# Attention, a Fourier mix and an MLP on one core: a second place for batch 0's scores, earlier transposes, another order of loads and weight sums

## The chip, the cores and the metric

The kernel runs on one core of one Trainium2 chip. The metric is the device time of one execution in microseconds (us), given as the median of several executions. A profile is taken of one execution; its times are counted from the start of that execution's span. The engines are PE (TensorE matmul, with PEld for its weight loads), DVE (VectorE), ACT (ScalarE), POOL (GpSimd) and SP (SyncE, which here issues DMAs only).

## The reference

The inputs are q, k and v of 4 batches, 8 heads, 768 positions and 64 channels, 8 memory keys and values for each head, and the two weights of an MLP. First comes attention in chunks, then a mix over positions and channels by Fourier transforms, then a normalised MLP:

```python
for c in range(768 // 32):                       # chunks of 32 queries
    k_ctx = k[:, :, max(0, 32*c - 16):min(768, 32*c + 40)]
    k_full = concat([mem_k, k_ctx]); v_full = concat([mem_v, v_ctx])
    a = softmax(q_c @ k_full.T / 8)
    out[:, :, chunk c] = a @ v_full
x = out as (4, 768, 512)
u = x + real(fft(fft(x, axis=1), axis=2))
un = (u - mean(u)) / sqrt(var(u) + 1e-6)
return u + relu(un @ w_ch1) @ w_ch2              # 512 -> 2048 -> 512
```

## The kernel before

**Work and tiles.** The heads are taken in pairs, n = 0 to 15, four pairs to a batch (`seq`, L250). One pair goes through these steps in `attention(n)` (L941):

- `e_load_qk` (L340) loads q and k from POOL's DMA queue and casts them to bf16, into one of three stage tiles `qs`, `ks` (L236, chosen by n modulo 3). `e_load_v` (L352) loads v from SP's queue into one of four tiles `va`, with a group of DMAs for each head: L362 for both heads' first keys, L358 for the others, L367 for the memory values. The tiles `va` have an edge set to zero and ones (`e_edges`, `e_edge_ones`) and low rows set to zero (`e_low_rows`, L329, an ACT copy).
- For batches 0 to 2, PE transposes q (`e_turn_q`, 16 matmuls of line L377 into the PSUM tile `trq`) and k (`e_turn_k`, into `trk`). `e_qT` (L393, ACT) copies the first to SBUF and `e_kT` (L412, line L420: DVE for pairs 0 to 3, ACT for 4 to 11) the second into `kTb`; `e_mkT` (L408) puts the memory keys there. For batch 3 DMA transposes do this.
- Each pair has two halves g. `e_scores` (L426, 12 matmuls of L433) writes the PSUM tile `sc`, of which there is one, two banks large. `e_exp` (L437, two ACT instructions of L441) reads it. `e_values` (L445, 24 matmuls of L457) multiplies with v into `xa` (g = 0) or a bank `xo` (g = 1). `e_norm` (L461, two DVE instructions, L467 and L468) divides and writes the batch's tile `xsb`.

After batch 0's pairs, `first_fourier` (L1071) makes folded sums on DVE (`g_zy` L599, `g_ff` L610 and others), splits them into high and low parts (L651 on ACT, L655 on DVE) and multiplies them with cosine and sine tables (L675, L688). `columns_of` (L1171) transforms the columns (L699), adds them to the batch's tile (`e_sum`, L705), takes mean and variance (L713, L714) and normalises (`e_un`). The MLP follows in tiles of 256 rows: first layer L775 with `e_relu` (L784), second layer L793, or for batches 2 and 3 a form with seven products of quarters instead of eight (L842) that needs sums of W2's quarters (`e_w2t`, L809 to L817, DVE).

**Order of the work.** All instructions are made as tasks of a planner (`Plan`, L37) and written out in the order that it finds. A task has an engine, an assumed cost, tasks that it comes after, PSUM banks or buffers that it takes and gives back, and a rank. At each planned moment each engine takes the ready task of lowest rank; without a rank of its own a task has its number, so batch 0's attention and its Fourier work come ahead of later pairs. `behind` holds a task until another has been placed. PE's costs are doubled before the planned time `WARM` (L44). The order is then fixed: on the chip each engine runs its list in order and waits where the data isn't there.

While PE has nothing ready, from the first scores up to the first low part of the Fourier work (L1120), the planner puts in products of zeros (`e_fill`, L899, matmul L902). They write a PSUM bank of their own, one of the two `mlp` banks. The PSUM banks in all: `tr` (1), `xa` (1), `sc` (2), `acc` (2), `mlp` (2).

**POOL's queue.** In order of rank: loads of pairs 0 to 2, memsets of the last rows of `ks` 1 and 2 (L885), masks, edges and ones of `va` 2 and 3, memsets of `kU` (L939), q and k of pair 3, and then a gate, a copy of one element of pair 3's v of head 1 (`e_gate`, L956), behind which the loads of pair 4 stand. The loads of W1 (L1062) come after pair 5's, those of W2 (L1067) after pair 6's.

Of the kernel before, what the change touches and what calls it, by code (L numbers as in the profile page):

```python
# [10 lines left out]
FP32 = mybir.dt.float32  # L11
# [25 lines left out]
class Plan:  # L37
# [6 lines left out]
    WARM = 18.0  # L44
# [47 lines left out]
    def order(self):  # L92
# [9 lines left out]
        while any(waiting.values()):  # L102
# [5 lines left out]
            for e, ts_ in waiting.items():  # L108
# [49 lines left out]
                else:  # L158
                    if e == "PE" and self.filling and self.filling[0]["at"] is not None \
                            and self.filling[1]["at"] is None:  # L160
                        cost = self.FILL * (2.0 if now < self.WARM else 1.0)
                        idle[e] = now + cost
                        placed.append(dict(engine="PE", cost=cost, emit=self.fill, at=now,
                                           done=now + cost))
                        moved = True
# [12 lines left out]
def kernel(  # L178
# [38 lines left out]

    bank_of, bank_free = {}, {"acc": [0, 1], "mlp": [0, 1]}

    def bank(tag, shape, dtype, name):  # L220
        i = bank_free[tag].pop(0)
        t = fps.tile(shape, dtype, tag=f"{tag}{i}", bufs=1, name=name)
        bank_of[name].append((t, tag, i)) if name in bank_of else bank_of.update({name: [(t, tag, i)]})
        return t
# [12 lines left out]
    ks = [spool.tile([P, 2, RB * D], BF16, name=f"ks{i}") for i in range(NS)]  # L237
    NV = 4
# [90 lines left out]
    def e_low_rows(i):  # L329
        low = va[i][0:MEM0].rearrange("p h t c -> p (h t c)")  # L330
        nc.scalar.copy(low, zero[0:MEM0].to_broadcast([MEM0, 2 * NT * 66]))
# [8 lines left out]
    def e_load_qk(n, i):  # L340
        b, pr = seq[n]
        src, dst = ((q, qs), (k, ks))[i]
        if b >= TURNED:
            for hh in range(2):
                nc.gpsimd.dma_start(
                    strided(dst[n % NS], hh * D, [[2 * D, NST], [1, D]]),
                    src[b, 2 * pr + hh].rearrange("(a p) d -> p a d", p=P))
            return
        nc.gpsimd.dma_start(dst[n % NS][0:QP],
# [30 lines left out]
    def e_flip_q(n):  # L380
        qT_of[n] = qT = apool.tile([P, S], BF16, tag="qT", bufs=2, name="qT")
        nc.sync.dma_start_transpose(qT.rearrange("p (a s) -> p a s", s=P),
                                    qs[n % NS].rearrange("p h c -> p (h c)")[:, 0:S])

    def e_flip_k(n):
        nc.sync.dma_start_transpose(kU[n % NKU][:, KR:KR + S].rearrange("p (a s) -> p a s", s=P),
                                    ks[n % NS].rearrange("p h c -> p (h c)")[:, 0:S])

    def e_turn_q(n):
        tr_of[n] = trq = aps.tile([P, S], BF16, tag="tr", bufs=1, name="trq")  # L390
        turn(trq, qs[n % NS][0:QP], ident_b[0:QP, 0:QP])

    def e_qT(n):  # L393
        qT_of[n] = qT = apool.tile([P, S], BF16, tag="qT", bufs=2, name="qT")
        nc.scalar.copy(qT.rearrange("p (a j) -> p a j", j=RB),  # L395
                       tr_of.pop(n).rearrange("p (j a) -> p a j", j=RB))

    def e_turn_k(n):
        if n < HP:
            trk = bank("acc", [P, RB * KP], BF16, "trk")  # L400
        else:
            trk = aps.tile([P, RB * KP], BF16, tag="tr", bufs=1, name="trk")
        tr_of[n, 1] = trk
        turn(trk, ks[n % NS][0:KP], turn_b)
# [21 lines left out]
    def e_scores(n, g):  # L426
        qT, kT = qT_of[n], kTb[n % NKT]
        sc_of[n, g] = sc = aps.tile([P, 2, 8, 64], FP32, tag="sc", bufs=1, name="sc")
# [448 lines left out]
    def e_idb():  # L877
# [7 lines left out]
    t_kzs = add("POOL", 1.0, lambda: [nc.gpsimd.memset(ks[i][QP:KP], 0.0) for i in range(1, NS)],  # L885
                rank=14)
    t_low, LOW = {}, 110
    for i in range(NV):
# [3 lines left out]
        t_low[i] = add("ACT", 1.45, lambda i=i: e_low_rows(i), [t_zero, e_],  # L892
                       rank=(0, 1, 2, 3)[i])
    t_masks = add("POOL", 0.6, e_masks, rank=16)
    dz = cpool.tile([P, P], BF16)
    fill_of = []
    t_dz = add("DVE", 0.15, lambda: nc.vector.memset(dz, 0.0), rank=-30)

    def e_fill():  # L899
        if not fill_of:  # L900
            fill_of.append(bank("mlp", [P, 512], FP32, "idle"))
        nc.tensor.matmul(fill_of[0][:, 0:384], dz, strided(dz, 0, [[0, 3], [1, P]]),  # L902
                         start=True, stop=True)

    t_fill = add("PE", 0.33, e_fill, [t_dz], take=("mlp",), rank=-1)
# [35 lines left out]
    def attention(n):  # L941
# [4 lines left out]
                      take=(("qs", "ks")[i],), moved=3.1 if b >= TURNED else 1.2, grain=0.032 if b >= TURNED else 0.1, late=LATE if b else 2.0,  # L946
                      behind=t_gate if n == HP else t_xr[b - 2] if n == TURNED * HP else t_ck.get(n - 1),
                      rank={0: -4 + i, 1: -1.2 + 0.1 * i, 2: 10 + 0.1 * i}.get(n)) for i in range(2)]
# [5 lines left out]
        if n == HP - 1:  # L954
            def e_gate():
                nc.gpsimd.tensor_copy(gate[64:65], va[n % NV][64:65, 1, NT - 1, 0:1])  # L956
# [10 lines left out]
        else:  # L967
            tq = add("PE", 0.40, lambda: e_turn_q(n), [lq, t_idb], take=("tr",), give=("qs",))
            dve = ("DVE", nc.vector.tensor_copy) if n < HP else ("ACT", None)
            eq = add("ACT", 0.80, lambda: e_qT(n), [tq], take=("qT",), give=("tr",),  # L970
                     rank=SINES - 0.5 if n == 0 else None)
            ktag = "acc" if first else "tr"
            tk = add("PE", 0.43, lambda: e_turn_k(n), [lk, t_idb, t_kz if n == 0 else t_kzs],
                     take=(ktag,), give=("ks",))
            ek = add(dve[0], 1.25 if dve[1] else 1.04, lambda: e_kT(n, dve[1]), [tk, mk],
                     give=(ktag,))
        xs_ = []
        for g in range(2):
            s_ = add("PE", 0.32, lambda g=g: e_scores(n, g), [eq, ek], take=("sc",),
# [3 lines left out]
                     [s_, t_masks, t_after.get(n)], take=("e1",), give=("sc",))  # L983
# [65 lines left out]
    for i in range(2, NV):  # L1049
        t_low[i]["behind"] = t_exp[i - 2, 1]  # L1050
        t_low[i]["rank"] = t_exp[i - 2, 1]["rank"] + 0.1
# [19 lines left out]
    def first_fourier():  # L1071
        t_rest, t_mid, t_row, pre = {}, {}, {}, {}
        for g in range(2):
# [28 lines left out]
            for par in range(2):  # L1102
                for ab in range(2):
# [15 lines left out]
                    if (par, ab, g) == (0, 0, 0):  # L1119
                        plan.filling = (t_sc[0, 0], add("PE", 0.0, lambda: let_go(fill_of[0]), [lo],  # L1120
                                                        give=("mlp",)))
# [48 lines left out]

    def columns_of(b, t_rest):  # L1171
# [33 lines left out]
        for i, kt in enumerate(kts):  # L1205
# [12 lines left out]
            sa = add("DVE", 0.9, lambda kt=kt: e_stats(b, kt), [su, sa])  # L1218
            if b in EVEN:
# [26 lines left out]
    def weight_sums(plain_end):  # L1246
        for i in range(4):
            t_sums.append(add("DVE", 1.2, lambda i=i: e_w2t(i),
                              [t_w2[3], plain_end if i == 3 else None] + side_end + t_sums[-1:],
                              rank=MLPS + len(plan.tasks)))  # L1250
# [109 lines left out]
    for b in range(1, B):  # L1360
        for i in range(HP):
            attention(b * HP + i)
            if b == 1 and i in (1, 2):
# [38 lines left out]
```

## Time and profile before

| quantity | value |
|---|---|
| median of 3 executions | 282.46 us (281.37 to 285.58) |
| profiled execution | 282.55 us, span 280.7 us |
| busy: PE, DVE, ACT, POOL | 264.3, 193.5, 155.2, 64.3 us |
| zero products (L902) | 29, median 0.326 us |
| first scores, last normalisation of batch 0 | 12.93 us, 32.66 us |
| first product of the MLP's first layer (L775) | 57.1 us |

How to read what follows. The page's digits give the busy share of each fortieth of the span in tenths. A row of the view by stages gives a stretch, its length, the busy time of PE, PEld, DVE, ACT and POOL with instruction counts, PE's granted clock, the DMA engines' share and GB/s. A row of the timeline gives the start, the duration, the engine and line, the tile written and the tiles read, the shapes, and in brackets the idle time before it and what ended it. A row of the chain gives start, length and what the chain was in.

### The profile page before, as it was taken

The numbers are of one execution on the slowest core, as the hardware profiler recorded it, in microseconds if no ns is written. First come the engines' busy times: TensorE is split into PE (matmuls) and PEld (weight loads), VectorE is DVE, ScalarE is ACT, GpSimd is POOL, SyncE is SP. The second block draws the span as 40 slices with busy tenths as digits, with TensorE's granted clock in tenths as the row PEclk, the third lists the DMA queues.
The fourth block names the chain that finished last, engine by engine and source line by source line (L and its number), as shares of the span: only waits on it lengthen the run. The fifth ranks groups of instructions, "written<-read, shape, count | busy, mean of one in ns | idle before, by whom it ended". The sixth has DMA issues, their size and how long they took to land.

```text
span 280.7 us, 7981 instructions
## 1 busy us (share of the span) xinstructions
PE 264.3 (94%) x3325; PEld 207.4 (74%) x3325; DVE 193.5 (69%) x424; ACT 155.2 (55%) x262; POOL 64.3 (23%) x127
## 2 busy tenths in 40 slices
PE   0589999999999999998999999999999999999995
PEld 0466698788756579766668766858988888888884
DVE  7968978970218979899688776599869825353444
ACT  6887667579665757734745665525526270605150
POOL 8840853240111038306200230101004100000000
PEclk9999999999999999999999999999999999999999
DMA  6989999999899969999999734497101507103152
GB/s 102 199 143 174 162 206 204 196 198 201 162 190 236 214 103 220 177 142 144 235 191 209 177 74 109 108 207 167 48 37 58 131 21 168 40 37 77 50 103 76
DMA packets 116116, 39.98 MB, mean 142 GB/s; under 512 B 104560, under 2 KB 111472, under 8 KB 116080
## 3 DMA queue, kind: packets, MB, share of 16 engines
q1 hardware_dynamic: 93888, 23.54, 46.9%
q0 software_dynamic: 21472, 15.21, 34.0%
q10 hardware_dynamic: 720, 0.72, 0.7%
q8 instruction: 26, 0.43, 0.7%
q14 instruction: 10, 0.08, 0.1%
HBM read 37.36 MB, written 13.37 MB: 181 GB/s over the span
## 4 chain that ended last, share of the span: by engine, by line
PE 84%; DMA 7%; DVE 4%; SPq 3%; issue 1%; POOL 0%; POOLq 0%
PE ph L775 31%; PE pc L793 15%; PE pc L842 13%; DMA va<-in_v_dram 6%; PE ps L529 6%; PE xa L457 4%; PE pm L699 4%; PE ps L688 3%; PE xo L457 3%; PE sc L433 2%; SPq L358 2%; DMA qs<-in_q_dram 1%; PE trk L377 1%; PE trq L377 1%; DVE xsb L705 1%; PE pm L580 1%
## 5 line engine op out<-in xcount | busy, mean ns | idle before, releaser
L775 PE MATMUL ph<-unT,w_sb 128*128 128x256 f16 x768 | 90.3, 273 | 0.8 <-DVE xsb L800 0.8
L784 ACT ACTIVATE hT<-ph 128x512 f16<-128x512 f32 x96 | 56.9, 598 | 54.3 <-PE pc L842 30.2
L775 PEld LDWEIGHTS <-w_sb 128*128 128x128 f16 x768 | 73.2, 98 | 11.1 <-issue 1.7
L793 PE MATMUL pc<-w_sb,hT 128*128 128x512 f16 x192 | 44.8, 380 | 0.0
L441 ACT ACTIVATE e<-sc,mbias 128x384 f32<-128x384 f32 x64 | 33.6, 576 | 19.0 <-PE sc L433 19.0
L793 PEld LDWEIGHTS <-hT 128*128 128x128 f16 x192 | 17.7, 98 | 19.0 <-issue 0.2
L847 DVE TENSOR_TENSOR xsb<-pc,xsb 128x256 f32<-128x256 f32 x43 | 18.0, 421 | 12.4 <-PE pc L842 10.6
L842 PEld LDWEIGHTS <-hT 128*128 128x128 f16 x240 | 23.3, 98 | 4.2 <-DVE hT L830 1.0
L842 PE MATMUL pc<-w_sb,hT 128*128 128x256 f16 x192 | 24.1, 272 | 0.5 <-DVE hT L830 0.5
L541 ACT CAST up<-ps 128x386 f16<-128x386 f32 x16 | 9.7, 605 | 17.6 <-PE ps L529 17.0
L830 DVE TENSOR_TENSOR S<-hT 128x768 f16<-128x768 f16 (+1 forms) x12 | 5.1, 422 | 18.5 <-ACT hT L784 17.9
L800 DVE SCALAR_TENSOR_TENSOR xsb<-pc,rstd,xsb 128x512 f32<-128x512 f32 x12 | 9.0, 750 | 12.2 <-PE pc L793 12.1
L713 DVE BATCH_NORM_STATS2 st<-xsb 128x6 f32<-128x512 f32 x24 | 16.6, 690 | 0.6
L705 DVE TENSOR_TENSOR xsb<-pm,xsb 128x512 f32<-128x512 f32 x15 | 10.2, 678 | 7.1 <-PE pm L699 6.9
L457 PEld LDWEIGHTS xa<-va,e 128*64 128x64 f32 x384 | 12.5, 137 | 3.2 <-issue 2.0
L457 PE MATMUL xa<-va,e 128*64 128x65 f32 x384 | 14.7, 226 | 0.0
L433 PEld LDWEIGHTS <-kTb 64*128 64x128 bf16 x384 | 7.8, 96 | 9.0 <-issue 8.1
L457 PE MATMUL xo<-va,e 128*64 128x65 f32 x384 | 14.1, 223 | 0.0
L546 DVE TENSOR_TENSOR up<-ps,up 128x386 f16<-128x386 f32 x16 | 9.6, 602 | 6.1 <-ACT up L541 6.1
L395 ACT COPY qT<-trq 128x768 bf16<-128x768 bf16 x12 | 9.5, 793 | 6.4 <-PE trq L377 6.4
L572 POOL DMA_DIRECT2D xr<-x_back x3 | 2.3, 770 | 46.7 <-DMA x_back<-x_rows 46.7
L519 DVE TENSOR_TENSOR lo<-ff,hi 128x768 f16<-128x768 f32 x12 | 11.3, 954 | 2.4 <-ACT hi L514 2.4
(168 smaller groups left out, 455.3 us busy)
## 6 DMA issues: line engine op xcount, KB each, us to landing
va<-in_v_dram SPq DMA_DIRECT2D x32, 220.0 KB
w_sb<-in_moe_w_ch_dram POOLq DMA_DIRECT2D x8, 512.0 KB, 16.9
out_dram<-xsb SPq DMA_DIRECT2D x12, 256.0 KB
qs<-in_q_dram POOLq DMA_DIRECT2D x12, 192.0 KB, 6.5
ks<-in_k_dram POOLq DMA_DIRECT2D x12, 192.0 KB, 7.0
x_rows<-xsb POOLq DMA_DIRECT2D x3, 768.0 KB, 4.6
xr<-x_back POOLq DMA_DIRECT2D x3, 768.0 KB, 5.0
out_rows<-xsb SPq DMA_DIRECT2D x9, 256.0 KB
```

The lines of the kernel that those rows point to most:

```text
L433: nc.tensor.matmul(sc[:, hh, t6, :], kT[r0:r0 + 64, t, :], qT[r0:r0 + 64, ts(t, 64)], start=True, stop=True, tile_position=(r0, 0))
L441: nc.scalar.activation(e1[:, :, :, ts(half, 32)], sc[:, :, 0:6, ts(half, 32)], AFT.Exp, bias=mbias[:, half:half + 1], scale=1.0 / math.sqr ...
L457: nc.tensor.matmul(xa[64 * half:64 * half + 64, st, hh, 0:65], e1[:, hh, t6, :], v1[:, hh, 6 * g + t6, 0:65], start=True, stop=True)
L519: nc.vector.tensor_tensor(lo[:, ab].rearrange(fl), ff_of[b, par][:, ab].rearrange(fl), hi[:, ab].rearrange(fl), ALU.subtract)
L529: nc.tensor.matmul(out_[:, sp, :], part[:, ab, sp * 3 + st, c0:c1], tab[:, sp, st, :], start=(st == 0 and i == 0), stop=(st == 2 and i == 1))
L705: nc.vector.tensor_tensor(uv, pm_of[b, kt], uv, ALU.add)
L713: nc.vector.bn_stats(st6, xs[b][:, kt, :])
L775: nc.tensor.matmul(ph[:, k, :], w1_sb[:, dt, ts(HH * k + i, P)], unT_of[b, j][:, dt, :], start=(dt == 0), stop=(dt == NDT - 1))
L784: nc.scalar.activation(hT_of[b, j][:, :, i, :], ph, AFT.Relu, bias=0.0, scale=1.0 if b in EVEN else -1.0)
L793: nc.tensor.matmul(pc_of[b, j, r], hT_of[b, j][:, k, i, ts(r, P)], w2_sb[:, HH * k + i, :], start=(i + k == 0), stop=(i + k == HH))
L842: nc.tensor.matmul(pc_of[key], a[:, i, :], w[:, i, :], start=(i == 0 and new), stop=(i == HH - 1), skip_group_check=not new)
L847: nc.vector.tensor_tensor(u, pc, u, ALU.add)
```

## The change

- Batch 0's scores of the second half (g = 1) go into the two `acc` banks, which are now one tile `accs` for the whole kernel. `trk` of batch 0 goes into an `mlp` bank instead of `acc`.
- The transposes of pairs 1 to 3 and their copies get ranks just below the scores of the pair before.
- Zero products start with the first one, at the start of the kernel, and go into any bank that is free (`mlp`, `tr` or `xa`), which they give back. `WARM` is 6 instead of 18.
- Pair 3's q and k get a stage tile of their own (`last_qk`), are loaded straight after pair 2's, and the memsets of the last rows of k are single tasks. The low rows of `va` 2 and 3 are memsets on POOL instead of ACT copies. The gate reads head 0 of pair 3's v. W2 is loaded after pair 7's q and k.
- `e_kT` of pairs 5, 6 and 7 is on DVE instead of ACT.
- The sums of W2 wait until the last statistics of batch 2 have been placed.

```diff
-    WARM = 18.0
+    WARM = 6.0
...
-                        cost = self.FILL * (2.0 if now < self.WARM else 1.0)
-                        idle[e] = now + cost
-                        placed.append(dict(engine="PE", cost=cost, emit=self.fill, at=now,
-                                           done=now + cost))
-                        moved = True
+                        tag = next((x for x in ("mlp", "tr", "xa") if self.free[x] > 0), None)
+                        if tag:
+                            cost = self.FILL * (2.0 if now < self.WARM else 1.0)
+                            idle[e] = now + cost
+                            self.free[tag] -= 1
+                            gives.append((now + cost, tag))
+                            placed.append(dict(engine="PE", cost=cost, at=now, done=now + cost,
+                                               emit=lambda tag=tag: self.fill(tag)))
+                            moved = True
...
+    accs = fps.tile([P, 2, 512], FP32, tag="acc", bufs=1, name="accs")
...
-        t = fps.tile(shape, dtype, tag=f"{tag}{i}", bufs=1, name=name)
+        if tag == "acc":
+            dims = [[math.prod(shape[j + 1:]), n] for j, n in enumerate(shape)][1:]
+            t = strided(accs[:, i, :], 0, dims)
+        else:
+            t = fps.tile(shape, dtype, tag=f"{tag}{i}", bufs=1, name=name)
...
+    last_qk = wpool.tile([P, 2, 2, RB * D], BF16, tag="w2t", bufs=1, name="last_qk")
+
+    def stage(n):
+        if n == H // 2 - 1:
+            return last_qk[:, 0], last_qk[:, 1]
+        i = (n - (n >= H // 2)) % NS
+        return qs[i], ks[i]
...
-        nc.scalar.copy(low, zero[0:MEM0].to_broadcast([MEM0, 2 * NT * 66]))
+        if i < 2:
+            nc.scalar.copy(low, zero[0:MEM0].to_broadcast([MEM0, 2 * NT * 66]))
+        else:
+            nc.gpsimd.memset(low, 0.0)
...
+    KDVE, QDVE = (5, 6, 7), ()
...
-        if n < HP:
-            trk = bank("acc", [P, RB * KP], BF16, "trk")
-        else:
-            trk = aps.tile([P, RB * KP], BF16, tag="tr", bufs=1, name="trk")
-        tr_of[n, 1] = trk
-        turn(trk, ks[n % NS][0:KP], turn_b)
+        tr_of[n, 1] = trk = (bank("mlp", [P, RB * KP], BF16, "trk") if n < HP else
+                             aps.tile([P, RB * KP], BF16, tag="tr", bufs=1, name="trk"))
+        turn(trk, stage(n)[1][0:KP], turn_b)
...
-        sc_of[n, g] = sc = aps.tile([P, 2, 8, 64], FP32, tag="sc", bufs=1, name="sc")
+        sc_of[n, g] = sc = (accs.rearrange("p h (t q) -> p h t q", q=64) if n < HP and g == 1 else
+                            aps.tile([P, 2, 8, 64], FP32, tag="sc", bufs=1, name="sc"))
...
-    t_kzs = add("POOL", 1.0, lambda: [nc.gpsimd.memset(ks[i][QP:KP], 0.0) for i in range(1, NS)],
-                rank=14)
+    t_kzs = [t_kz] + [add("POOL", 1.0, lambda i=i: nc.gpsimd.memset(stage(i)[1][QP:KP], 0.0),
+                          rank=r) for i, r in ((1, 14), (2, 17.05), (3, 17.15))]
...
-        t_low[i] = add("ACT", 1.45, lambda i=i: e_low_rows(i), [t_zero, e_],
-                       rank=(0, 1, 2, 3)[i])
+        t_low[i] = add("ACT" if i < 2 else "POOL", 1.45 if i < 2 else 1.7, lambda i=i: e_low_rows(i), [t_zero, e_],
+                       rank=(0, 1, 17.3, 17.4)[i])
...
-                      take=(("qs", "ks")[i],), moved=3.1 if b >= TURNED else 1.2, grain=0.032 if b >= TURNED else 0.1, late=LATE if b else 2.0,
+                      take=(("qs", "ks")[i],) if n != HP - 1 else (), moved=3.1 if b >= TURNED else 1.2, grain=0.032 if b >= TURNED else 0.1, late=LATE if b else 2.0,
...
-                      rank={0: -4 + i, 1: -1.2 + 0.1 * i, 2: 10 + 0.1 * i}.get(n)) for i in range(2)]
+                      rank={0: -4 + i, 1: -1.2 + 0.1 * i, 2: 10 + 0.1 * i, 3: 10.2 + 0.1 * i}.get(n)) for i in range(2)]
...
-                nc.gpsimd.tensor_copy(gate[64:65], va[n % NV][64:65, 1, NT - 1, 0:1])
+                nc.gpsimd.tensor_copy(gate[64:65], va[n % NV][64:65, 0, NT - 1, 0:1])
...
-            dve = ("DVE", nc.vector.tensor_copy) if n < HP else ("ACT", None)
+            ahead = [None if b or n == 0 else t_sc[n - 1, 0]["rank"] - 0.9 + 0.1 * i for i in range(4)]
...
+            dve = ("DVE", nc.vector.tensor_copy) if n < HP or n in KDVE else ("ACT", None)
...
-            ktag = "acc" if first else "tr"
+            ktag = "mlp" if first else "tr"
...
+        xs_, sct = [], (("sc",), ("acc", "acc") if first else ("sc",))
...
-            s_ = add("PE", 0.32, lambda g=g: e_scores(n, g), [eq, ek], take=("sc",),
+            s_ = add("PE", 0.32, lambda g=g: e_scores(n, g), [eq, ek], take=sct[g],
...
-                        plan.filling = (t_sc[0, 0], add("PE", 0.0, lambda: let_go(fill_of[0]), [lo],
-                                                        give=("mlp",)))
+                        plan.filling = (t_fill, add("PE", 0.0, lambda: None, [lo]))
...
-                              rank=MLPS + len(plan.tasks)))
+                              rank=MLPS + len(plan.tasks), behind=t_stats[2, 5]))
...
-            if b == 1 and i in (1, 2):
+            if b == 1 and i in (1, 3):
                 weights(b * HP + i)
```

The ranks in `ahead` go, in this order, to the transpose of q, its copy, the transpose of k and its copy.

## The prediction

> **What bounds the kernel now.** I read the page's 40 slices and its chain first, then the busy time by stage, then the chain in order of time up to 60 us, then the instructions of 24 to 30 and of 47 to 50 us.
>
> ```profile
> PE   0589999999999999998999999999999999999995
> ...
> DVE  7968978970218979899688776599869825353444
> ...
> PE 84%; DMA 7%; DVE 4%; SPq 3%; issue 1%; POOL 0%; POOLq 0%
> ```
>
> The reader is to see that TensorE is short of work only in the first slices (7 us each), that DVE stands at 7 to 9 tenths in most of them too, and that of the share that is not PE in the chain, DMA and SPq (10%) stand nearly all there. The same by stage:
>
> ```profile
> 13.00:33.00 20.00, 18.45 (x411) 13.28 (x412) 16.11 (x42) 14.98 (x31) 8.55 (x23) 1.00 0.96 158
> 33.00:58.00 25.00, 24.35 (x401) 21.25 (x399) 21.86 (x52) 15.68 (x30) 10.51 (x18) 1.00 1.16 201
> 58.00:281.00 223.00, 218.19 (x2468) 170.60 (x2465) 144.12 (x297) 115.03 (x192) 34.02 (x56) 1.00 0.77 134
> ```
>
> The columns after the length are PE, PEld, DVE, ACT and POOL. From 33 us on PE is full. In 13 to 33 its 18.45 us hold zero products (29 in the whole run, 0.326 us median), so only time saved before about 33 us, where PE waits for batch 0's attention, moves the end. What that stage waits for:
>
> ```profile
> 15.88 4.83 DMA va<-in_v_dram
> 20.73 1.77 SPq L358
> 22.90 4.40 DMA va<-in_v_dram
> 27.98 4.19 DMA qs<-in_q_dram
> ```
>
> The second half of pair 3's v, issued at 22.90, is there at 27.3; the gate on POOL (L956) lets pair 4's q go only then. Beside this chain runs a second one, the single score tile:
>
> ```profile
> 25.24 0.35 PE L433 MATMUL sc<-qT,kTb 64*128 64x64 bf16 x12
> ...
> 25.69 1.05 ACT L441 ACTIVATE e<-sc,mbias 128x384 f32<-128x384 f32 x2 [1.13 <-PE sc L433]
> ...
> 27.13 0.35 PE L433 MATMUL sc<-qT,kTb 64*128 64x64 bf16 x12
> ...
> 27.58 1.05 ACT L441 ACTIVATE e<-sc,mbias 128x384 f32<-128x384 f32 x2 [0.83 <-PE sc L433]
> ```
>
> Scores and exponentials alternate, 1.9 us a turn, and ACT waits for PE each time. The last exponential of batch 0 ends at 30.52, the last normalisation (L468) at 32.66. From there the Fourier products start.
>
> **The change, part by part.**
>
> *Scores, turns ahead, low rows.* With a second score place, ACT no longer alternates with PE. It also loses two zero copies of 1.5 us (L331 at 17.49 and 21.45). From the end of the table switch at 13.83, ACT then has eight pairs of exponentials of 1.04 and three qT copies of 0.78: 10.7 us, so it could be done at 24.5 in place of 30.52. It is no longer last. Two others are next:
> - v of pair 3. DMA moved 190 GB/s in 8 to 15 us, 88 in 15 to 17, 163 in 17 to 20. The lost (2 x 102 + 3 x 27 =) 285 KB are 1.5 us at 190. The q and k of pair 3 (384 KB) move from 16.54 to about 9.3, ahead of the memsets on POOL, and can fill that hole. So v is there at 25.8, not 27.3. Values of both halves and the last normalisation take 2.6 us from there (xa 0.71 ahead of xo; from xo's start at 30.90 to 32.66 are 1.76): 28.4.
> - DVE. Between 14.90 (tables done) and 32.66 it is busy 13.96 of 17.76 us. The same work packed without a gap ends at 28.86. The first gaps, 16.0 to 18.9, stand behind pair 0's exponentials, of which the second can come about 0.9 earlier only; I leave 0.6 of the 3.8 us idle: 29.46.
>
> DVE is the later, so the front gains 32.66 - 29.46 = 3.2 us. Bounds: 3.8 (no DVE gap) and 1.5: the work on v's edges now stands behind two more issues (1.3 us) on POOL, and if this puts v of pair 3 at 28.5, its last norm ends at 31.1.
>
> *Moved on POOL.* Order now: q3, k3, ks1 memset (1.03), masks, edges, ks2 memset, ones, last k's memset, two low memsets, kU. The ones of pair 2 come at about 15.7 instead of 14.4; SP, still issuing v of pair 1 until 15.07, then waits 0.6, inside the bounds above. The low memsets of 32x1584 f32: the nearest rows are 128x800 in 0.77 and 4x1024 in 1.03, about 1 ns an element, so 1.6 each, done near 20.5. Values of pair 2 can't start before v at about 22, so they are covered; uncovered they would cost 1.6. A kT copy beside POOL's kU memsets (14.81) took 1.18, others 1.25: no slowing seen, price 0.
>
> The Trainium skill, page "SBUF — State Buffer", section "SBUF: two separate sides", speaks against this move: a GpSimd operation and certain VectorE operations hold one shared port pair exclusively, and the other blocks for the whole instruction. No row here shows a VectorE copy held by a memset. By the page, as an estimate, the two low memsets could hold DVE up to 3.2 us, and the sum would stand at 283.6 instead of 280.4.
>
> *Gate and loads.* The gate now asks for head 0 of pair 3, whose issue (19.46) is 3.4 us earlier. q4 and k4 (384 KB) may then run beside v's second half: inside the bounds. Queued behind the gate on POOL are q4 to k5 and the mid products; only DMA waits for it. w2's four issues are moved behind q7 and k7: 384 KB at 200 GB/s delay w2 by 1.9 us. The last w2 issue is at 45.31, landing takes at most 21.3: 66.6, with the delay 68.5, and L793 wants w2 at 75.7 (72.5 in the new time). Covered by 4 us. Pair 7's turns, at 72.02 and 74.32 now, come earlier.
>
> *kT of pairs 5 to 7 on DVE.* 1.25 each (the DVE row of L420) where ACT took 1.04. Here is the place:
>
> ```profile
> 47.51 1.04 ACT L420 COPY kTb<-trk 128x1056 bf16<-128x1056 bf16 x1 [0.97 <-PE trk L377]
> ...
> 47.75 0.56 DVE L468 TENSOR_TENSOR xsb<-xo,zs 128x384 f32<-128x384 f32 x1
> ...
> 48.48 0.69 DVE L705 TENSOR_TENSOR xsb<-pm,xsb 128x512 f32<-128x512 f32 x1 [0.17 <-PE pm L699]
> ```
>
> Pair 5's copy stood on ACT just ahead of batch 0's chain of sums and statistics, in which DVE is busy 8.50 of 9 us (48 to 57) and PE waits for it. On DVE it fits the 0.17 us before 48.48 only by pushing the chain: 1.25 - 0.17 = +1.1. Below: 0, if it lies in DVE's gap at 40 to 43. Above: 2.3, if it is put behind the chain, since the scores and values of pair 5 (0.7 + 1.6 us of PE), which fill PE at 50 to 57, then have nothing in their place. Pairs 6 and 7 fall where DVE is idle (0.73 busy of 7 us in 63 to 70): 0.
>
> *W2 sums.* Three of 1.22 us, at 110.3, 113.3 and 151.1, go behind 167.2 (the last statistics of batch 2). Products with them start at 201.6, and DVE is idle 6.5 us in 168 to 196: price 0; with that cover gone, 3.7. What they leave at 110 to 114 is worth nothing, as the sum at 115.67 waits 1.11 for PE.
>
> *Zero products in any bank, from 1 us on.* The transposes of a pair took 0.85 us up to 12.06 and 0.53 from 17.93, after PE had run without a stop for some 5 us; started at 1 us, the fast state should be there at q0's turn, 8.95. That shortens PE by 0.3 a turn where it waits for DMA anyway: 0. A product can wait for the last reader of its bank, with all of PE behind it: 0 to 1.1, the time by which scores lagged at 25.24 behind an exponential ended at 23.88; I take 0, as 22 of them from 20 us on waited for nothing.
>
> *Sum.* The profiled execution took 282.55 us (span 280.7). 282.55 - 3.2 + 1.1 = 280.45. The median of the three runs, 282.46, is 0.1 lower: 280.4.
>
> **The rivals.**
> - *The transfer hides it.* v of pair 3 lands at 28.5: the front gains 1.5, the kT copy takes 1.1: 282.1. For it: DMA's share is 0.96 in 13 to 33. Against: the hole at 15 to 17.
> - *DVE becomes the bound* (slower). Place: 45 to 58 us. DVE has 3.1 us free in 33 to 58; kT 5 and kT 6 take 2.5. If kT 5 lands behind the chain (2.3) and kT 6, whose turn moves from 58.94 to about 56, inside it (1.25), that is 3.6; it decides from 3.2 up. Time 282.9, and up to 284.5 where fewer front gaps close (gain 1.6). Against: DVE's work of batch 0 has precedence in the planner.
> - *It does not do what it says.* The order is fixed by planned times; zero products, which PE must run through, keep scores at their planned place, as at 25.24. Then nothing is gained: 282.5 + 0.5.
> - *More.* All DVE gaps close (3.8), kT 5 costs nothing, and PE's wait at 128.09 (0.76) goes as pair 7 is earlier: 278.0.
>
> **How the numbers follow.** Forecast 0.52 (279.2 to 281.7), hidden 0.16, DVE 0.13, no effect 0.07, more 0.12. The range takes in "more" with 0.5 of margin and the slower rival's upper end: 277.5 to 284.5. 2% of 282.46 is 5.6 us, about what can be told from no change. Faster by that (under 276.8) needs more than any priced gap of the front, 0.07; slower (over 288.1) needs several uncovered costs, 0.05; 0.88 within.
>
> **What would show it.** Right: no wait of the exponentials for sc in 13 to 30 us; the last norm of batch 0 near 29.5; first row products (L688; 35.0 now) near 31.8; kT 5 on DVE close ahead of the first sum (L705); first L775 near 55 instead of 57.1; everything later shifted by 2 us. Wrong: v of pair 3 after 28 us, or the first L775 at 57 or later. The forecast fails most easily if the shift at 57 us is lost or grows behind it, where I count PE as full.

## The result, and the profile after

The changed kernel takes 294.61 us (median of 4 executions, 294.6 to 299.89) against 282.07 us of the kernel before beside it: 1.042 times the time, 95% interval 1.031 to 1.053. The forecast was 280.4 with a range to 284.5, so it is outside, on the slow side.

In the execution profiled with the result PE stood for 2.2 us at 30.5 us and had a granted clock of 0.50 from 33 to 39 us after it, and it took 299.89 us; so the profile is read from one more execution of the same kernel (run a1_again, 295.34 us, span 293.3). Line numbers are those of the changed kernel: zero products L921, scores L453, exponentials L461, values L477, norms L487 and L488, column products L719, their sum L725, first MLP layer L795.

The page's digits and its chain:

```profile
PE   8899999799999999998998999999999889999995
...
DVE  7849977871446795697786479468688588162534
...
PE 75%; DVE 15%; ACT 6%; issue 3%; POOL 0%; ACTq 0%; DVEq 0%; POOLq 0%
```

PE is now busy from the first slice (zero products), and DMA and SPq, 10% of the chain before, are gone from it. But DVE holds 15% of the chain in place of 4, ACT 6%. The same by stage:

```profile
13.00:33.00 20.00, 18.80 (x412) 12.92 (x412) 14.23 (x40) 12.38 (x25) 11.45 (x25) 1.00 0.92 168
33.00:58.00 25.00, 22.88 (x324) 19.39 (x323) 19.96 (x46) 12.69 (x26) 10.49 (x17) 1.00 1.13 194
58.00:294.00 236.00, 224.03 (x2564) 174.08 (x2561) 152.78 (x310) 115.03 (x195) 34.54 (x56) 1.00 0.70 126
```

In 33 to 58 us PE is busy 22.88 us instead of 24.35 and does 324 matmuls instead of 401, although nothing of DVE's or ACT's work has grown there. What it waits for in the whole run is in the view of PE's waits (engine, line, tile; the total, the count, the longest):

```profile
PE accs L719 <- DVE xsb L725: 1.3, 2, 0.8
PE accs L549 <- ACT hT L804: 1.2, 2, 0.7
PE accs L795 <- DVE xsb L725: 1.2, 2, 0.6
...
PE accs L862 <- DVE up L566: 0.8, 1, 0.8
PE accs L600 <- DVE xsb L725: 0.6, 1, 0.6
```

In the kernel before, the same view has one wait of PE for an accumulator bank:

```profile
PE pm L699 <- DVE xsb L705: 0.7, 2, 0.5
```

Every row shown of the changed kernel is the shared tile `accs`; all its rows together are 7.8 us, and of the rows not shown for other tiles none is over 1.0. The pairs make no sense as data: row products of a later batch (L549) wait for a relu of an earlier one, products of the MLP's first layer (L795) for a sum of column products. The two halves of the tile hold unrelated work; if the tile is the cause, a write to one half waits for the reader of the other. Run a2_two tests that.

To follow where time goes I use one more number, PE's **lag**: from the trace's records of matmuls, zero products left out and each counted at its length in columns, the moment at which PE has done a given amount of work, less the same moment in the kernel before. In a1_again the lag is +0.4 us at 25.7 us, +1.1 at 34, +4.0 at 56, +5.2 at 106, +8.3 at 176, +12.4 at 233, and +12.6 at the end. A lag of 2.9 us at 18.6 us is made up by 25.7; so little is left of it in the front, and then a little comes in every Fourier stage.

### The profile page after: what moved, and what is told of

It reads as the page before. It is cut to its first block, busy times and chain, and to the rows that moved or that the text cites. A ratio compares the mean times of both kernels' runs of the same rounds, so it can differ in the third digit from the quotient of the medians.

```text
span 297.9 us, 8070 instructions
## 1 busy us (share of the span) xinstructions
PE 278.6 (94%) x3366; PEld 212.0 (71%) x3366; DVE 198.6 (67%) x427; ACT 149.2 (50%) x257; POOL 67.7 (23%) x130
## 4 chain that ended last, share of the span: by engine, by line
PE 75%; DVE 15%; ACT 5%; issue 4%; POOL 0%; ACTq 0%; DVEq 0%; POOLq 0%
PE ph L795 17%; PE pc L813 14%; PE pc L862 7%; PE accs L795 5%; PE accs L549 5%; PE xa L477 4%; PE accs L719 4%; PE idle L921 4%; PE xo L477 3%; ACT hT L804 3%; DVE xsb L725 2%; PE accs L862 2%; PE sc L453 2%; DVE st L733 2%; PE trq L397 2%
## 5 line engine op out<-in xcount | busy, mean ns | idle before, releaser
L795 PEld LDWEIGHTS <-w_sb 128*128 128x128 f16 x768 | 74.2, 98 | 15.3 <-issue 5.2
L795 PE MATMUL ph<-unT,w_sb 128*128 128x256 f16 x584 | 70.2, 273 | 1.3 <-DVE xsb L820 0.8
L804 ACT ACTIVATE hT<-ph 128x512 f16<-128x512 f32 x73 | 43.3, 598 | 50.0 <-PE ph L795 25.1
L461 ACT ACTIVATE e<-sc,mbias 128x384 f32<-128x384 f32 x56 | 29.5, 580 | 16.1 <-PE sc L453 16.0
L795 PE MATMUL accs<-unT,w_sb 128*128 128x256 f16 x184 | 23.7, 272 | 2.5 <-DVE xsb L725 1.2
L804 ACT ACTIVATE hT<-accs 128x512 f16<-128x512 f32 x23 | 13.6, 598 | 18.6 <-PE accs L795 6.2
L921 PE MATMUL idle<-dz 128*128 128x384 bf16 x70 | 19.7, 387 | 2.0 <-DVE zero L307 1.0
L862 PE MATMUL pc<-w_sb,hT 128*128 128x256 f16 x136 | 18.3, 273 | 0.5 <-DVE hT L850 0.4
L561 ACT CAST up<-accs 128x386 f16<-128x386 f32 x14 | 8.3, 602 | 17.4 <-PE accs L549 7.4
L725 DVE TENSOR_TENSOR xsb<-accs,xsb 128x512 f32<-128x512 f32 x15 | 10.2, 681 | 8.2 <-PE accs L719 7.4
L477 PEld LDWEIGHTS xa<-va,e 128*64 128x64 f32 x384 | 12.5, 137 | 3.8 <-issue 2.7
L921 PEld LDWEIGHTS <-dz 128*128 128x128 bf16 x70 | 7.0, 110 | 11.1 <-issue 7.6
L477 PE MATMUL xa<-va,e 128*64 128x65 f32 x384 | 14.6, 226 | 0.0
L566 DVE TENSOR_TENSOR up<-accs,up 128x386 f16<-128x386 f32 x14 | 8.2, 594 | 9.2 <-ACT up L561 4.6
```

The source lines that it names most:

```text
L461: nc.scalar.activation(e1[:, :, :, ts(half, 32)], sc[:, :, 0:6, ts(half, 32)], AFT.Exp, bias=mbias[:, half:half + 1], scale=1.0 / math.sqr ...
L477: nc.tensor.matmul(xa[64 * half:64 * half + 64, st, hh, 0:65], e1[:, hh, t6, :], v1[:, hh, 6 * g + t6, 0:65], start=True, stop=True)
L725: nc.vector.tensor_tensor(uv, pm_of[b, kt], uv, ALU.add)
L795: nc.tensor.matmul(ph[:, k, :], w1_sb[:, dt, ts(HH * k + i, P)], unT_of[b, j][:, dt, :], start=(dt == 0), stop=(dt == NDT - 1))
L804: nc.scalar.activation(hT_of[b, j][:, :, i, :], ph, AFT.Relu, bias=0.0, scale=1.0 if b in EVEN else -1.0)
L862: nc.tensor.matmul(pc_of[key], a[:, i, :], w[:, i, :], start=(i == 0 and new), stop=(i == HH - 1), skip_group_check=not new)
```

## The experiments

**The changed kernel again, two tiles, a dearer zero product, and both.** Three theories: one tile ties the two banks (1); zero products cost more than planned (2); the new order itself is worse (3).

Run a1_again is the changed kernel as it is, once more.

> The changed kernel once more, to have its profile at a granted clock of 1.0 throughout (the profiled run of it, 299.9 us, had a clock of 0.5 from about 32.5 to 39 us). All theories: 294.6 us, span 292.6. If the shared accumulator tile is the cause (theory 1), the column products (L719) of the later bank still start only after the sum (L725) of the earlier one, and PE's lag behind the kernel before is under 2 us at the first row products and grows by some 10 us in the Fourier stages and the MLPs behind it.

Measured: 295.34 us, clock 1.0. The lag did as theory 1 said. The timeline of the column products shows the tie:

```profile
49.64 0.38 PE L719 MATMUL accs<-nsinD,up 128*128 128x256 f16 x2
50.06 0.69 DVE L725 TENSOR_TENSOR xsb<-accs,xsb 128x512 f32<-128x512 f32 x1 [0.65 <-PE accs L719]
51.61 0.66 DVE L725 TENSOR_TENSOR xsb<-accs,xsb 128x512 f32<-128x512 f32 x1
52.32 0.38 PE L719 MATMUL accs<-cosD,up 128*128 128x256 f16 x2 [0.75 <-DVE xsb L725]
...
60.39 0.69 DVE L725 TENSOR_TENSOR xsb<-accs,xsb 128x512 f32<-128x512 f32 x1 [0.78 <-ACT hT L804]
```

Two sets of products run, up to 50 us, before the first sum starts; both sums are read before PE starts the third set, at 52.32. At 60.39 a sum on DVE waits for a relu on ACT that reads the other half.

Run a2_two:

```diff
-        if tag == "acc":
-            dims = [[math.prod(shape[j + 1:]), n] for j, n in enumerate(shape)][1:]
-            t = strided(accs[:, i, :], 0, dims)
-        else:
-            t = fps.tile(shape, dtype, tag=f"{tag}{i}", bufs=1, name=name)
+        t = fps.tile(shape, dtype, tag=f"{tag}{i}", bufs=1, name=name)
...
+        sc_of[n, g] = sc = ([bank("acc", [P, 8, 64], FP32, "sc") for _ in range(2)] if n < HP and g == 1
```

> The two accumulator banks are two tiles again, and batch 0's scores of the second half take both, so that its exponentials are four instructions instead of two; PE's order of instructions is that of the changed kernel. Theory 1 (one tile for two banks ties each write of one bank to the reads of the other, so that PE and DVE take turns): the lag that grows in the Fourier stages goes, about 10 us of the 12, so 283 to 286 us. Theory 2 (a zero product takes 0.32 us and more in place of the planned 0.17, PE falls behind its plan, and the order doesn't fit afterwards): no gain, 293 to 296. Theory 3 (the order itself: kT copies on DVE, W2's sums and loads later): no gain either, 293 to 296.

Measured: 284.32 us, ratio to the kernel before 1.007 (1.003 to 1.011). Theory 1 holds, theory 3 falls: 10.3 us less with the same order of instructions on PE. Both ways of making the halves, here and in b1_one below, are raw access patterns into the tile (`strided`); whether ordinary slices of it would wait less was not run. The same place in its timeline:

```profile
48.17 0.38 PE L719 MATMUL pm<-nsinD,up 128*128 128x256 f16 x2
48.19 0.68 DVE L725 TENSOR_TENSOR xsb<-pm,xsb 128x512 f32<-128x512 f32 x1
48.39 0.38 PE L719 MATMUL pm<-cosD,up 128*128 128x256 f16 x2
```

The sum of the first set runs beside the products of the second, as before. PE's lag is 0.5 us at 34 us, stays under 2.5 from there on and is 1.6 at the end: the growth is gone.

Runs a3_fill and a4_both (the second with two tiles as well):

```diff
-    FILL = 0.17
+    FILL = 0.33
...
-                            cost = self.FILL * (2.0 if now < self.WARM else 1.0)
+                            cost = self.FILL
```

> Only the planner's price of a zero product is changed, from 0.17 to 0.33 us (the profile has 0.28 for one, 19.7 us for 70), so that fewer are placed and PE keeps its planned times; the shared accumulator tile stays. Theory 1: PE gains the 0.5 to 2 us that it lags at 26 us, and the rest of the loss stays: 292.5 to 295. Theory 2: most of the loss goes: 283 to 287. Theory 3: 293 to 296.

> Two accumulator tiles and zero products priced at 0.33 us. Theory 1: as the run with two tiles, less 0 to 2 us: 281 to 285 us; with it the front's gain that was forecast could show at last (280.4). Theory 2: as the run with the price alone, 283 to 287. Theory 3: 292 to 296.

Measured: a3_fill 293.95 us, ratio 1.041 (1.035 to 1.047), no gain to be told from the changed kernel. a4_both 281.23 us, ratio 0.996 (0.991 to 1.000). So the price of zero products, with the order that the planner makes of it, is worth 3.1 us (284.32 to 281.23), but only once the tie is gone; with it the lead of 2.1 us that a3_fill has at 34 us is lost again, a part of it in one wait of 2.88 us for a transpose of `un`. The front of a4_both is the one forecast:

```profile
26.02 0.80 PE L477 MATMUL xa<-va,e 128*64 128x65 f32 x20 [0.17 <-DMA va<-in_mem_v_dram]
...
27.79 0.56 DVE L488 TENSOR_TENSOR xsb<-xo,zs 128x384 f32<-128x384 f32 x1
```

Pair 3's v is there at 26.0, the last normalisation of batch 0 ends at 28.35 (27.79 and 0.56), before 32.66; PE leads by 3.4 us at 34 us and 2.8 at the end. The execution profiled here, 279.94 us, is the fastest of the eight.

**Each of the two costs alone, put into the kernel before.** b1_one makes the two accumulator banks halves of one tile there; b2_fill takes over only the zero products (from the start on, any bank, allocated anew, `WARM` 6).

> The kernel before with one edit: its two accumulator banks are one tile, of which each bank is a half; the order of instructions is that of the kernel before. If one tile is by itself what costs the 10 us (run a2_two), this kernel loses about as much: 291 to 295 us, and the second half's column products start only behind the first half's sum. If the tie of the banks costs only in the order of the changed kernel, it loses under 3 us: 282 to 285.

> The kernel before with one edit: zero products from the first one on, in any free bank, allocated anew for each, planned from 6 us on at 0.17 us. The kernel before leaves the profile's pitch of 0.162 us for that of 0.19 to 0.38. If the waits of zero products on their own bank put PE behind its plan (the changed kernel lagged by 2.7 us at the useful work that the kernel before reaches at 18.6 us), it loses 1 to 4 us: 283.5 to 286.5. If they only fill time in which PE waits anyway: 282 to 283.

Measured: b1_one 298.24 us, ratio 1.055 (1.050 to 1.060), more than I expected of it. PE's waits in it name the shared tile again:

```profile
PE accs L704 <- DVE xsb L710: 2.9, 4, 1.5
PE accs L847 <- DVE xsb L852: 1.8, 3, 0.8
PE accs L798 <- DVE xsb L594: 1.7, 2, 0.8
```

b2_fill 287.06 us, ratio 1.017 (1.011 to 1.023): 4.8 us. In its profiled execution (285.83) the lag is 2.8 us at 34 us and 3.3 at the end. Either edit alone makes the kernel before slower. How b2_fill's loss divides between waits and the plan was not taken apart.

**Is it the waits of the zero products?** When two follow each other in `tr` or `xa`, of which there is one bank, the second starts 0.38 us after the first in a1_again, 0.16 or 0.22 in `mlp`; in the kernel before it is 0.162 to 0.174 (all at full clock). Run a6b_keep takes the waits away and leaves the order of a2_two:

```diff
+        i = f"mlp{bank_free['mlp'][0]}" if tag == "mlp" else tag
+        if i not in idle_of:
+            idle_of[i] = (fps if tag == "mlp" else aps).tile([P, 512], FP32, tag=i, bufs=1, name="idle")
+        nc.tensor.matmul(idle_of[i][:, 0:384], dz, strided(dz, 0, [[0, 3], [1, P]]),
```

> Two accumulator tiles, the same order of instructions on every engine, but a zero product writes the tile of the zero product before it as long as nothing else has taken that bank, so that it has no release to wait for. In the run with two tiles alone, the start of one zero product to the next is 0.38 us where they follow each other in the tr or xa bank and 0.19 on average in the two mlp banks; in the kernel before it is 0.162. Theory 2 for what is left of the loss (the waits of zero products on their own bank hold PE behind its plan in the front): the pitch is 0.162 everywhere at full clock, the lag of 3.9 us against the run that has both repairs goes, 280 to 281.5 us. Rival: the number of zero products costs, 70 against 46, not their waits: no gain against two tiles alone, 283.5 to 285.

Measured: 285.36 us, ratio 1.015 (1.008 to 1.023). The pitch is 0.162 to 0.163 everywhere at full clock. Eight products in a row in a1_again,

```profile
16.02 2.77 PE L921 MATMUL idle<-dz 128*128 128x384 bf16 x8
```

and in a6b_keep:

```profile
15.04 1.47 PE L927 MATMUL idle<-dz 128*128 128x384 bf16 x8
```

But the time isn't less, and theory 2 as I had put it fails. PE leads by 1.9 us at 25.7 us and lags by 1.5 at 34, because of this:

```profile
26.21 0.34 PE L482 MATMUL xa<-va,e 128*64 128x65 f32 x4
28.97 1.35 PE L482 MATMUL xa<-va,e 128*64 128x65 f32 x20 [2.43 <-DMA va<-in_mem_v_dram]
30.91 1.57 PE L482 MATMUL xo<-va,e 128*64 128x65 f32 x24
```

Pair 3's v lands at 28.9 us. PE arrives 2.43 us early, and its clock falls: the 20 products take 1.35 us instead of 0.80, the 24 after them 1.57 instead of 0.92. That is the rival "the transfer hides it" (v at 28.5), by its mechanism. It also means that this run can't price the waits by themselves: its own standstill is in the result.

Run a10_keep33 has a4_both's order and no such waits, a11_late has two tiles and zero products only from the first scores on.

> Two accumulator tiles, a price of 0.33 us for a zero product (46 of them), and no wait for their own bank. In the run with 70 products without waits PE was 1.9 us ahead of the kernel before at 25.7 us, and then stood 2.43 us before the last pair's values, whose v landed at 28.9 us; in the run with both repairs (46, with waits) v was there at 26.0 and PE 3.4 us ahead at 34 us. If the fewer products are what lets the issue of v and its landing come early: 279 to 281.5. If it is chance in the transfers, or the waits helped: 283 to 285.

> Two accumulator tiles, and zero products only from the first scores on, as before, with costs doubled before 18 us of the plan, as before; they still go into any free bank and wait there. Tells how much of the difference of 3.1 us between the run with two tiles (284.3, 70 zero products) and the one with both repairs (281.2, 46) is in the early ones: if early products delay batch 0's transposes and scores, about 280 to 282; if the early warm clock is worth something, since transposes took 0.85 us in place of 0.53 without it, 283 to 285.

Measured: a10_keep33 282.82 us, ratio 1.001 (0.998 to 1.004); PE waits 2.10 us for pair 3's v, there at 27.3. Taking the waits away gained nothing, and fewer products did not by themselves bring v in early. a11_late 282.38 us, ratio 1.001 (0.997 to 1.005), between the two expectations: inconclusive.

**The gate.** d2_gate, d3_gate33 and d4_gate4 are a6b_keep, a10_keep33 and a4_both with one index changed; the order of instructions is the same.

```diff
-                nc.gpsimd.tensor_copy(gate[64:65], va[n % NV][64:65, 0, NT - 1, 0:1])
+                nc.gpsimd.tensor_copy(gate[64:65], va[n % NV][64:65, 1, NT - 1, 0:1])
```

> As a6b_keep, with the gate reading head 1 of pair 3's v again, as in the kernel before; the order of instructions is that of a6b_keep. There PE stood 2.43 us before the last pair's values for a landing of memory values at 28.9 us, 4.7 us after their issue, while q and k of pair 4 were issued from 26.16 on. If q and k of pair 4 take the transfers' time from pair 3's v: the landing comes 1 to 2 us earlier and the time is 282 to 284 us in place of 285.4. If v is late because of its own issue (24.2, against 22.6 in a4_both): no gain or a loss, 285 to 286.5.

> As a10_keep33 (46 zero products, none waits for its bank), with the gate at head 1 again, the order of instructions unchanged. There PE stood 2.10 us before the last pair's values for v, which landed at 27.3 us. If the early gate costs: 280 to 281.5. If not: 282.5 to 284.

> As a4_both (46 zero products, with waits), with the gate at head 1 again, the order of instructions unchanged. There v was nearly in time (PE waited 0.17 us), so the gate should make no difference by v: 280.5 to 282; a later q and k of pair 4 costs if their transposes at 35 us then wait: up to 283.

Measured: d2_gate 284.44 us, ratio 1.003 (0.999 to 1.007), where a6b_keep had 285.36 and 1.015; d3_gate33 281.23 us, 0.997 (0.994 to 0.999), where a10_keep33 had 282.82 and 1.001; d4_gate4 0.997 (0.994 to 1.001), where a4_both had 0.996. The twelve executions of d4_gate4 run from 279.77 to 287.70 us with a median of 283.17, so that pair settles little.

The wait for v is 1.68 us in d2_gate instead of 2.43, and 0.21 in d3_gate33 instead of 2.10. But an earlier v explains at most a part of this:

```profile
24.35 0.20 PE L457 MATMUL sc<-qT,kTb 64*128 64x64 bf16 x2 [1.15 <-issue]
...
27.31 0.80 PE L482 MATMUL xa<-va,e 128*64 128x65 f32 x20 [0.21 <-DMA va<-in_mem_v_dram]
```

In d3_gate33, shown here, v is there at 27.3 us, as in a10_keep33; PE only came to it later, after a pause of 1.15 us. What d3_gate33 was spared is the fall of the clock: 0.50 from 28.43 to 31.84 us in a10_keep33, none there. In the first pair v moved from 28.9 to 28.1. With the earlier gate v was there at 26.0 (a4_both), 27.3, 28.0 (d5_sums below, which has a4_both's order up to that point) and 28.9 us, with the later one at 27.3, 28.1 and 28.7 (e2_best below). So the runs do not show that the early gate makes v late; they show that v is there anywhere between 26.0 and 28.9 us.

d3_gate33 is the one version whose interval lies below 1 against the kernel before, by a third of a per cent; with this many versions tried, one such interval can be chance.

**The other parts.** a9_w2 is a6b_keep (which the expectations call a6_keep) with W2's sums and loads as before; d5_sums is a4_both with the sums early; e1_sums is the kernel before with the sums late.

> As a6_keep, with the sums of W2's quarters where their data allows (before, about 110 to 150 us) and the loads of W2 after pair 6 again. The prediction priced both moves at 0: within 0.5 us of a6_keep. Rival: sums of 1.2 us each between the column sums and statistics of batch 1 hold PE, slower than a6_keep by up to 2 us, or W2 later holds the first second-layer products, faster than a6_keep.

> As a4_both, with the three sums of W2's quarters where their data allows, in place of behind the last statistics of batch 2. The prediction priced the move at 0: within 0.6 us of a4_both, 280.6 to 281.8. If the early sums hold the column sums of batch 1, in which PE waits for DVE: 282 to 284, all of it between 105 and 155 us.

> The kernel before with one edit: the three sums of W2's quarters wait until the last statistics of batch 2 have been placed, as in the changed kernel. In d5_sums, with the sums early, PE lost some 1.5 us between 165 and 212 us that a4_both did not lose. If the move is worth that by itself: 280.5 to 281.5 us. If it is worth something only in the changed order, as the prediction's price of 0 says for this one: 281.8 to 282.8.

Measured: a9_w2 286.9 us, ratio 1.012 (1.006 to 1.017), not to be told from a6b_keep. d5_sums 284.49 us, ratio 1.008 (1.004 to 1.011), 3.3 us above a4_both. Its profiled execution is 4.75 us above that of a4_both: by the lag, 3.1 us are lost in the front, where the order is the same (v at 28.0 us), and 2.4 between 144 and 212 us, with some given back before and after. The sums themselves stand at 111 to 115 us there, where nothing is lost, so this is the order that the planner makes behind them, which neither expectation had. e1_sums 290.11 us, ratio 1.028 (1.024 to 1.033), all lost in one wait, with which no theory had reckoned:

```profile
133.85 8.96 PE L775 MATMUL ph<-unT,w_sb 128*128 128x256 f16 x64 [7.28 <-DMA unT<-un]
```

With the sums gone from there the planner puts the loads of a later pair's v on SP's queue ahead of five transposes of `un` (issued from 126.79 on; three of them from 123.69 on in the kernel before). The run says what the new order costs, not what the sums do.

a8_low is a6b_keep with ACT's low rows, a7_kact with all kT copies on ACT; e2_best is d3_gate33 with pair 5's alone on ACT.

> As a6_keep, with the low rows of v tiles 2 and 3 as ACT copies again, in their old places behind the exponentials of pairs 0 and 1. The prediction counted two copies of 1.5 us taken off ACT as part of what lets the exponentials end early, and 0 for the memsets on POOL. If ACT is the later engine in the front: slower than a6_keep by 1 to 3 us, 281.5 to 284. If ACT has room there (12.4 busy of 20 us in 13 to 33): within 0.5 us of a6_keep.

> As a6_keep, with the kT copies of pairs 5 to 7 on ACT again, as in the kernel before. The prediction priced their move to DVE at +1.1 us by 57 us and nothing later: so 1.1 us less than a6_keep, 279 to 280.5. Rival: the copies land where DVE has time (the column sums are not held by them), no difference, within 0.5 us of a6_keep; or the move helps ACT and this is slower than a6_keep.

> As d3_gate33, with the kT copy of pair 5 on ACT again, those of 6 and 7 still on DVE. In every run with pair 5's copy on DVE it stood behind batch 0's last column sum, and PE lost 0.4 to 0.5 us of its lead between 34 and 56 us; the prediction priced this at 1.1. If the copy is the reason: 0.4 to 1.1 us faster, 280.1 to 280.8. If the new order loses elsewhere (a7_kact, with all three on ACT, lost 9 us in a wait for a DMA transpose at 128 to 135 us): 282 or more.

Measured: a8_low 282.48 us, ratio 1.001 (0.997 to 1.005), faster than a6b_keep and against my expectation. Its last pair's values start at the same time (29.05 us) but without a wait for v, and 24 take 0.93 us where 20 took 1.35; zero products kept PE busy from 24.8 us to 26.9, and the clock stayed at 1.0. a7_kact 294.38 us, ratio 1.039 (1.034 to 1.044), again one wait for `un`'s transposes:

```profile
135.33 3.57 PE L800 MATMUL ph<-unT,w_sb 128*128 128x256 f16 x16 [7.48 <-DMA unT<-un]
```

Up to 56 us it tells about the copies, though: between 34 and 56 us its lag changes by -0.1 us, and by +0.4 in a9_w2, which has the same order up to 34 us. e2_best 288.88 us, ratio 1.022 (1.018 to 1.027): it waited 2.48 us for pair 3's v at 28.7 us and 2.22 more for a later pair's at 76.9. With pair 5's copy on ACT its lag changes by -0.4 us between 34 and 56 us, in d3_gate33 by +0.4. The prices of the copies and of the sums by themselves stay open beyond that; each edit moved too much of the order.

## Why the prediction was wrong

- **The accumulators' one tile** is the step that failed the forecast. The prediction's list of parts has no term for it at all: I followed what is written into `accs`, and took the two banks of it as two places, as they are in the planner. What the runs showed: a write to one half waits for the reader of the other, 10.3 us in the changed order, 16.0 us alone in the kernel before (298.24 less 282.26). The diff shows it in four lines, and the profile of before shows where the price is: the sum (L705) at 48.48, whose row the prediction shows, runs beside products of the next set, and that is what one tile forbids.

```profile
48.37 0.39 PE L699 MATMUL pm<-cosD,up 128*128 128x256 f16 x2
...
48.59 0.38 PE L699 MATMUL pm<-nsinD,up 128*128 128x256 f16 x2
```

- **Zero products in any bank**: the step "0 to 1.1, I take 0" was too small. 3.1 us between a2_two and a4_both, 4.8 us alone. I priced a wait for another reader of the bank and overlooked that a product would wait for the one before it (0.38 us a piece where two follow each other in `tr` or `xa`, planned at 0.17). That the waits as such are the loss is not shown: a6b_keep without them is no faster, and between 70 products planned at 0.17 and 46 at 0.33 the whole order differs.
- **The front's gain** of 3.2 us did not come in the changed kernel: its last normalisation of batch 0 ends at 31.86 us in a1_again, against 32.66 before and 29.46 in the forecast, and its first MLP product stands at 58.64, past the 57 that the prediction calls wrong. With both repairs, and where v came in time, the size was right: 3.4 us of lead at 34 us in a4_both. The exponentials hardly wait for scores any more (0.74 us at most from 20 us on, 1.13 before); in the changed kernel

```profile
24.01 1.06 ACT L461 ACTIVATE e<-sc,mbias 128x384 f32<-128x384 f32 x2
...
24.67 0.35 PE L453 MATMUL accs<-qT,kTb 64*128 64x64 bf16 x12
...
25.12 1.05 ACT L461 ACTIVATE e<-accs,mbias 128x384 f32<-128x384 f32 x2
```

  the scores of one half are written while the other is read. DVE closed even more gaps than I allowed (last norm at 28.35 against 29.46).
- **v of pair 3** at 25.8: 26.0 in a4_both, 27.3 to 28.9 in others. The forecast and its first rival each came true, in different executions, so a4_both's 26.0 is in part luck; 0.16 was too small a chance for a landing that varies by 2 to 3 us.
- **The gate**, "inside the bounds": 0.9 and 1.6 us by the medians of two pairs (a6b_keep and d2_gate, a10_keep33 and d3_gate33). That is inside, but by which way is not shown.
- **kT on DVE**, +1.1: the copy of pair 5 fell behind the chain of sums (55.59 in a4_both), as the upper bound had it, but cost about 0.5 in place of 2.3: between 34 and 56 us the lag changes by +0.4 in a4_both, a9_w2 and d3_gate33, and by -0.1 and -0.4 in a7_kact and e2_best, with that copy on ACT. It is not so in every run with the copy on DVE (+0.1 in a10_keep33, -0.5 in a8_low).
- **Memsets on POOL**, 0: those of the low rows took 2.77 us for two, against an estimate of 3.2, and the kT copy beside them was not held:

```profile
17.18 2.77 POOL L351 MEMSET va<- 32x1584 f32 x2
```

```profile
18.16 1.26 DVE L439 COPY kTb<-trk 128x1056 bf16<-128x1056 bf16 x1 [1.92 <-PE trk L397]
```

  1.26 us in a4_both, as for the copies at 14.89 and 21.10 with no low memset beside them. Those copies read PSUM. The small copy of the memory keys (L427), from SBUF to SBUF, was held:

```profile
16.06 0.18 DVE L427 COPY kTb<-mkT 128x96 bf16<-128x96 bf16 x1
...
19.89 1.46 POOL L960 MEMSET kU<- 128x800 bf16 x2
...
20.72 0.69 DVE L427 COPY kTb<-mkT 128x96 bf16<-128x96 bf16 x1
```

  It took 0.69 us in place of 0.18 and ended at 21.41, 0.05 after the memset (21.36). The same copy took 0.85 us in a6b_keep, with its end at 14.83 and that of a memset of `ks` at 14.78, and 0.72 in a11_late, 0.05 behind the end of a memset of the low rows. So what the Trainium skill, page "SBUF — State Buffer", section "SBUF: two separate sides", says of the shared port does show in this trace, on a copy that the prediction did not look at; the price was 0.5 to 0.7 us of DVE a time, not 0. Whether any of it reached the end of the kernel is not shown.
- **W2's sums**, 0: a4_both keeps its lead from 56 us (2.9) to the end (2.8), so all that was moved behind 56 us, this included, cost nothing in sum against the kernel before. No run isolates it.

With the two missed terms the sum is 280.4 + 10.3 + 3.1 = 293.8 us; measured 294.6. The two are steps of one path (294.61, 284.32, 281.23), so the sum says no more than that a4_both is 0.8 us above the forecast. By the other path, through a3_fill (293.95), the steps are 0.7 and 12.7: the two do not add up independently.

## What to carry to other kernels

Before two PSUM banks become one tile, look at what runs in them side by side: where products into one overlap a read of the other, as at 48.48 us here, one tile made the engines take turns, whatever the halves held. Filler work has a price: what it takes on the chip must be what the plan takes for it, and time gained by one engine is only worth what the next transfer allows. An experiment in a planned order should leave the order as it is; runs that let the planner place everything anew (a7_kact, e1_sums, e2_best) answered another question.

## What the runs showed of the hardware

A standstill of PE can cost more than its length, because the granted clock can fall with it. After 2.43 us in a6b_keep the granted clock was 0.74 in 28 to 30 us and 0.50 in 30 to 32; after 7.48 us in a7_kact 16 products took 3.57 us where 16 take 1.92 in the kernel before (57.09). The length alone does not decide: the clock also fell after 2.10 us (a10_keep33) and 1.68 us (d2_gate), and stayed at 1.00 after 1.76 us (a9_w2, at 26 us), 1.80 us (a11_late, at 125) and 2.22 us (d4_gate4, at 127).

Each of these falls lasted 3.41 us or a multiple of it: 28.94 to 32.36 in a6b_keep, 28.43 to 31.84 in a10_keep33, 29.68 to 33.09 in d2_gate, twice that in the result's profile (32.45 to 39.28, after 2.22 us) and three times in a7_kact (129.86 to 140.10). The Trainium skill, page "TensorE: Matmul & The Clock Gate", section "Part 1: The HAM clock gate", puts the fall to half clock after an idle window of about 3.4 us, and calls the window free-running. The fall to 0.50 and the step of 3.41 us agree; a standstill as long as the window was not needed here.

A memset on GpSimd held a small VectorE copy from SBUF to SBUF until 0.05 us after its end (0.69 us in place of 0.18 at 20.72 in a4_both), and did not hold copies from PSUM (1.26 us with and without).
